# Loading a 1.2 KB input on the SyncE queue behind a 5 MB weight, instead of on the ScalarE queue at the same time

## Chip, cores, metric

The kernel runs on one core of a Trainium2 chip. The metric is the device time of one execution in microseconds (us), median of several runs. Times inside a trace are us from the start of the span.

## The reference, cut to what matters

One decode step of a transformer block: attention over a cache and a gated feed-forward, both on the layernormed input, summed with the input.

```python
x  = A_x                                     # [1, 1, 640] bf16: 1.2 KB
xn = layernorm(x)
# A: 32 heads, head size 128, 32768 cached positions each
q  = xn @ wq                                 # wq [640, 4096]: 5 MB
p  = softmax(q · k_cache * 128**-0.5)        # k_cache: 32 heads x 8 MB
A  = (p @ v_cache) @ wo                      # v_cache: 32 heads x 8 MB
# B: (silu(xn @ w_gate) * (xn @ w_up)) @ w_down
out = x + A + B
```

Nearly all of the 554 MB that the kernel reads is the cache. Loading it needs nothing of x, but no score can be computed before q.

## The kernel before

Every large input goes through a ring of three slots in SBUF. SyncE issues all large loads in one fixed order: wq, k0, k1, v0, k2, v1, ... (k0 is the k cache of head 0), then the feed-forward weights and wo. A load is issued as soon as its slot's last user is done. wq takes slot 0, k0 slot 1, k1 slot 2, and v0 takes slot 0 again: it waits until the q matmuls have read wq.

```python
ahead(lambda: nc.sync.dma_start(wq, A_wq...).then_inc(s_wq, 16))          # ahead of the start barrier
ahead(lambda: nc.scalar.dma_start(xrow, A_x[0, 0:1, :]).then_inc(s_x, 16))
...
@block.sync                                                               # after the start barrier
def sp(e):
    owner = {}                                                            # slot -> (semaphore, count) that frees it
    for u in units:
        s = slot_of[u]
        if s in owner:
            e.wait_ge(*owner.pop(s))
        if u[0] == "wq":
            owner[s] = (s_q, NQB)                                         # freed by the 8 groups of q matmuls
        elif u[0] == "k":
            e.dma_start(ring[:, s, :], kv_src(A_k_cache, u[1], 0, NJ)).then_inc(s_slot[s], 16)
            owner[s] = (s_qk, NHF * (u[1] + 1))                           # freed by that head's score matmuls
        ...
        elif u[0] == "v":
            e.dma_start(ring[:, s, :], kv_src(A_v_cache, u[1], 0, NJ)).then_inc(s_slot[s], 16)
            owner[s] = (s_pv, u[1] + 1)
```

xrow lies in the unused part of slot 0, on one partition. The layernorm runs on PE, DVE and ACT; its last step is a DVE copy that spreads xn for the matmuls. Then come the q matmuls, the copies of q from PSUM on ACT, and the first multiply:

```python
@block.tensor
def pe(t):
    t.wait_ge(s_x, 16)
    ... # two transposes of x, two sums of the layernorm
    t.wait_ge(s_a, 11)                     # DVE: xn is spread
    t.wait_ge(s_wq, 16)
    for b in range(NQB):                   # NQB = 8
        for c in range(NCD):
            mm = t.matmul(bank[b], lhsT=xnb[:, c, :], rhs=wq_v[:, c, b * 512:(b + 1) * 512], ...)
        mm.then_inc(s_q, 1)
    t.wait_ge(s_qc, NQB)                   # ACT: all 8 copies of q done
    ... # head after head: scores, softmax sums, p @ v

@block.vector
def dve(v):
    ... # layernorm
    step(v.tensor_copy(out=xnb[:, :, :], in_=xn[:, :, None].to_broadcast([128, NCD, 128])))
    v.wait_ge(s_qc, 1)                     # ACT: first copy of q done
    ... # per head: wait for its k load, four multiplies k * q, reductions, softmax
```

Of the kernel before, what the change touches and what calls it, by code (L numbers as in the profile page):

```python
# [12 lines left out]
def bass_parallel_sum__gqa_block_cached__swiglu_ffn__decode_kernel(  # L13
# [65 lines left out]
    with ExitStack() as es:  # L79
# [3 lines left out]
        def sem(name):  # L83
            return es.enter_context(nc.semaphore(name))
# [33 lines left out]
        s_x, s_wq, s_out = sem("x"), sem("wq"), sem("o")  # L118
# [20 lines left out]
        xrow = flat[0:1, x0 + NCD * 128:x0 + NCD * 128 + D]  # L139
# [5 lines left out]
        def ahead(start):  # L145

            at_start = nc.main_func.blocks[0]
            n = len(at_start.instructions)
            start()
            ins = list(at_start.instructions)  # L150
            new = ins[n:]
            drain = next(i for i, x in enumerate(ins)
                         if x.engine == new[0].engine and type(x).__name__ == "InstDrain")
            at_start.instructions = ins[:drain] + new + ins[drain:n]

        ahead(lambda: nc.sync.dma_start(wq, A_wq.rearrange("(p c) n -> p (c n)", c=NCD)).then_inc(s_wq, 16))
        ahead(lambda: nc.scalar.dma_start(xrow, A_x[0, 0:1, :]).then_inc(s_x, 16))
        block = es.enter_context(nc.Block(no_gpsimd_drain=True))
        f0 = FFN_S * CE
        wg = flat[:, f0:f0 + NCD * F]  # L160
# [23 lines left out]
        def kv_src(cache, h, j0, n):  # L184
            return cache[0, h].rearrange("(p j) d -> p (j d)", p=128)[:, j0 * DH:(j0 + n) * DH]
# [20 lines left out]
        with nc.psum_tensor("ps8", [128, 8, 512], F32) as ps8:  # L206
# [10 lines left out]
            @block.sync  # L217
            def sp(e):
                owner = {}
                for u in units:  # L220
                    s = slot_of[u]
                    if s in owner:
                        e.wait_ge(*owner.pop(s))
                    if u[0] == "wq":
                        owner[s] = (s_q, NQB)
                    elif u[0] == "k":
                        e.dma_start(ring[:, s, :], kv_src(A_k_cache, u[1], 0, NJ)).then_inc(s_slot[s], 16)
                        owner[s] = (s_qk, NHF * (u[1] + 1))
                    elif u == LASTV:
                        j = 0  # L230
                        for i, n in enumerate(TAIL):
                            e.dma_start(ring[:, s, j * DH:(j + n) * DH],
                                        kv_src(A_v_cache, u[1], j, n)).then_inc(s_tail[i], 16)
                            j += n
# [3 lines that stand above are left out]
                    elif u[0] == "ffn":  # L238
                        e.dma_start(wg, B_w_gate.rearrange("(p c) n -> p (c n)", c=NCD)).then_inc(s_ffn[0], 16)
                        e.dma_start(wu, B_w_up.rearrange("(p c) n -> p (c n)", c=NCD)).then_inc(s_ffn[1], 16)  # L240
                        e.dma_start(flat[:, d0:d0 + FM * D], B_w_down[0:FM * 128, :].rearrange(
                            "(p j) n -> p (j n)", j=FM)).then_inc(s_ffn[2], 16)
                        e.dma_start(wdr, B_w_down[FM * 128:F, :].rearrange(
                            "f (t n) -> (f t) n", t=2)).then_inc(s_ffn[2], 16)
                    else:
                        wo_src = A_wo.rearrange("(p j) n -> p (j n)", j=OC)
                        j = 0
                        for i, n in enumerate(WTAIL):
                            e.dma_start(wo[:, j * D:(j + n) * D], wo_src[:, j * D:(j + n) * D]).then_inc(s_wo[i], 16)  # L249
                            j += n  # L250
                e.wait_ge(s_fin, 2)
                e.dma_start(out[0, 0:1, :].rearrange("o (c m) -> (o c) m", c=NCD), orow[:, :]).then_inc(s_out, 16)
# [399 lines left out]
```

## Time and profile before

| | before |
|---|---|
| time, median of 3 runs | 1287.27 us (1287.13 to 1287.53) |
| span of the profiled execution | 1285.6 us |
| read from memory | 554 MB, 431 GB/s over the span |
| busy: PE, DVE, ACT | 81%, 52%, 4% |

First the top of the profile page of before: busy time by engine (share of the span), then 40 equal slices of the span with the busy share of the DMA engines in tenths. PE is TensorE's matmuls, PEld its weight loads, DVE is VectorE, ACT ScalarE, POOL GpSimd; in the timelines SPq and ACTq are DMA issues of SyncE and ScalarE.

```profile
PE 1042.0 (81%) x5154; PEld 260.9 (20%) x3235; DVE 672.2 (52%) x409; ACT 52.1 (4%) x139; POOL 2.5 (0%) x17
...
DMA  9999999999999999999999999999999999999998
```

The DMA engines are at nine tenths or more in 39 of 40 slices. The compute engines are not full.

The start is where the change acts. The timeline of before gives, for each row: start in us, length in us, engine, source line, operation, and in brackets how long the engine had been idle and what ended that.

```profile
0.00 0.40 SPq L156 DMA_DIRECT2D ring<-in_A_wq_dram  x1
0.12 0.51 ACTq L157 DMA_DIRECT2D ring<-in_A_x_dram  x1
...
1.06 1.10 SPq L227 DMA_DIRECT2D ring<-in_A_k_cache_dram  x2
...
1.58 0.33 PE L282 MATMUL ps<-one,ring 1*128 1x1 bf16 x5 [1.58 <-DVE one L516]
...
5.67 0.82 DVE L535 COPY ring<-xn 128x640 bf16<-128x640 bf16 x1
...
15.35 10.43 PE L297 MATMUL ps<-ring 128*128 128x512 bf16 x39 [10.75 <-DMA ring<-in_A_wq_dram]
...
25.80 0.33 SPq L236 DMA_DIRECT2D ring<-in_A_v_cache_dram  x1
...
34.67 17.43 DVE L554 TENSOR_TENSOR ring<-ring,qb 128x8192 bf16<-128x8192 bf16 x4 [28.19 <-DMA ring<-in_A_k_cache_dram]
```

x is used from 1.58 us on. The layernorm runs while wq is being loaded and ends at 6.49 us. The q matmuls wait for wq until 15.35 us. v0 is issued at 25.80 us, when the q matmuls are done. The first multiply waits for k0 until 34.67 us: "idle 28.19" is the wait of DVE.

### The profile page before, as it was taken

The numbers are of one execution on the slowest core, as the hardware profiler recorded it, in microseconds if no ns is written. First come the engines' busy times: TensorE is split into PE (matmuls) and PEld (weight loads), VectorE is DVE, ScalarE is ACT, GpSimd is POOL, SyncE is SP. The second block draws the span as 40 slices with busy tenths as digits, with TensorE's granted clock in tenths as the row PEclk, the third lists the DMA queues.
The fourth block names the chain that finished last, engine by engine and source line by source line (L and its number), as shares of the span: only waits on it lengthen the run. The fifth ranks groups of instructions, "written<-read, shape, count | busy, mean of one in ns | idle before, by whom it ended". The sixth has DMA issues, their size and how long they took to land.

```text
span 1285.6 us, 9851 instructions
## 1 busy us (share of the span) xinstructions
PE 1042.0 (81%) x5154; PEld 260.9 (20%) x3235; DVE 672.2 (52%) x409; ACT 52.1 (4%) x139; POOL 2.5 (0%) x17
## 2 busy tenths in 40 slices
PE   3599777889787799778788777898777798778797
PEld 1012112221112221112221112221112221112227
DVE  0855665445665446664446664446664446654441
ACT  2000000000000000000000000000000000000000
POOL 0000000000000000000000000000000000000000
PEclk9799888999888898888998888998888998888995
DMA  9999999999999999999999999999999999999998
GB/s 424 425 445 433 427 430 441 428 432 440 432 432 428 440 430 430 442 430 432 428 440 430 430 442 430 432 428 440 430 430 442 430 432 428 440 430 430 442 413 365
DMA packets 11256, 554.17 MB, mean 431 GB/s; under 512 B 1259, under 2 KB 1516, under 8 KB 1772
## 3 DMA queue, kind: packets, MB, share of 16 engines
q1 hardware_dynamic: 11242, 554.00, 99.7%
q8 instruction: 9, 0.15, 0.0%
q14 instruction: 3, 0.02, 0.0%
q10 hardware_dynamic: 2, 0.00, 0.0%
HBM read 553.99 MB, written 0.00 MB: 431 GB/s over the span
## 4 chain that ended last, share of the span: by engine, by line
DMA 53%; PE 28%; DVE 12%; issue 6%; SPq 0%; DVEq 0%
DMA ring<-in_A_k_cache_dram 51%; PE ps L337 17%; DVE ring L554 12%; PE ps L305 9%; DMA ring<-in_A_wo_dram 2%; PE ps L324 1%; PE ps L379 0%; PE ps L373 0%; PE ps L367 0%; PE ps L428 0%; SPq L249 0%; DVEq L554 0%; DVE sc L560 0%; DVE pmax L566 0%; DVE m L569 0%
## 5 line engine op out<-in xcount | busy, mean ns | idle before, releaser
L554 DVE TENSOR_TENSOR ring<-ring,qb 128x8192 bf16<-128x8192 bf16 x128 | 557.8, 4420 | 315.6 <-DMA ring<-in_A_k_cache_dram 315.6
L305 PE MATMUL ps<-ring,ident 128*128 128x512 bf16 x1920 | 498.4, 418 | 0.0
L337 PE MATMUL ps<-ring,P 128*4 128x512 bf16 x1984 | 443.3, 379 | 0.0
L324 PE MATMUL ps<-ring,ident 128*128 128x512 bf16 x128 | 56.1, 439 | 220.1 <-DVE ring L554 219.7
L337 PEld LDWEIGHTS ps<-ring,P 128*4 128x4 bf16 x1984 | 163.4, 85 | 237.8
L324 PEld LDWEIGHTS ps<-ring,ident 128*128 128x128 bf16 x128 | 12.6, 99 | 618.3 <-DVE ring L554 359.5
L560 DVE TENSOR_REDUCE sc<-ps 128x64 f32<-128x512 f32 x128 | 82.2, 683 | 63.4 <-PE ps L305 63.4
L572 DVE TENSOR_SCALAR negb<-ps 128x1 f32<-128x1 f32 x32 | 5.1, 159 | 108.4 <-PE ps L379 108.4
L480 ACT ACTIVATE P<-sc,negb 128x256 bf16<-128x256 f32 x32 | 16.2, 507 | 957.7 <-DVE negb L572 957.7
L569 DVE TENSOR_REDUCE m<-ps 1x1 f32<-1x128 f32 x32 | 8.9, 279 | 85.2 <-PE ps L373 85.2
L359 PEld LDWEIGHTS ps<-identf,o 4*128 4x128 f32 x248 | 30.7, 190 | 13.1 <-issue 13.1
L359 PE MATMUL ps<-identf,o 4*128 4x1 f32 x248 | 33.3, 251 | 0.0
L367 PEld LDWEIGHTS ps<-rsum,ones 128*128 128x128 f32 x64 | 12.1, 190 | 99.7 <-issue 98.9
L471 ACT ACTIVATE o<-ps,rzb 4x512 f32<-4x512 f32 x31 | 21.0, 678 | 6.2 <-PE ps L337 6.2
L297 PE MATMUL ps<-ring 128*128 128x512 bf16 x39 | 10.4, 428 | 10.8 <-DMA ring<-in_A_wq_dram 10.7
L476 ACT ACTIVATE ocol<-ps 128x1 f32 (+1 forms) x31 | 5.4, 173 | 222.4 <-PE ps L359 222.4
L566 DVE TENSOR_REDUCE pmax<-sc 128x1 f32<-128x256 f32 x32 | 13.4, 420 | 0.0
L373 PE MATMUL ps<-identf,pmax 128*1 128x128 f32 x64 | 12.2, 273 | 1.2 <-DVE pmax L566 1.2
L379 PE MATMUL ps<-m,ones 1*128 1x1 f32 x64 | 12.1, 256 | 0.4 <-DVE m L569 0.4
L379 PEld LDWEIGHTS ps<-m,ones 1*128 1x128 f32 x64 | 9.4, 182 | 14.2 <-issue 13.5
L403 PE MATMUL ps<-xn,ring 128*128 128x1 bf16 x140 | 8.3, 196 | 1.3 <-issue 1.3
L542 DVE RECIPROCAL rzb<-ps 128x1 f32<-128x1 f32 x32 | 5.0, 157 | 8.1 <-PE ps L367 8.1
(66 smaller groups left out, 82.5 us busy)
## 6 DMA issues: line engine op xcount, KB each, us to landing
ring<-in_A_wq_dram SPq DMA_DIRECT2D x1, 5120.0 KB, 15.2
ring<-in_A_v_cache_dram SPq DMA_DIRECT2D x1, 4096.0 KB, 31.8
ring<-in_A_wo_dram SPq DMA_DIRECT2D x3, 1280.0 KB, 24.7
ring<-in_B_w_gate_dram SPq DMA_DIRECT2D x1, 2160.0 KB, 23.2
ring<-in_B_w_up_dram SPq DMA_DIRECT2D x1, 2160.0 KB, 27.9
ring<-in_B_w_down_dram SPq DMA_DIRECT2D x1, 2080.0 KB, 31.3
ring<-in_A_v_cache_dram SPq DMA_DIRECT2D x1, 2048.0 KB, 36.4
ring<-in_A_v_cache_dram SPq DMA_DIRECT2D x2, 1024.0 KB, 39.4
```

The source lines that it names most:

```text
L305: return t.add_instruction(mybir.InstMatmult(start_tensor_calc=False, stop_tensor_calc=stop, tile_size=(128, 128), tile_position=(0, 0), l ...
L324: t.matmul(ob, lhsT=ident[:, :], rhs=src, start=True, stop=False)
L337: mm = t.matmul(O, lhsT=P[:, h % PR, j:j + W], rhs=ring[:, s, j * DH:(j + W) * DH], start=(j == 0), stop=(j + W == NJ))
L359: mm = t.matmul(fold_ps, lhsT=o4[:, m * DH:(m + 1) * DH], rhs=identf[0:W, m:m + 1], start=(m == 0), stop=(m == W - 1))
L367: t.matmul(misc[:, 129:130], lhsT=ones[:, :], rhs=rsum[:, h % SR:h % SR + 1], start=True, stop=True).then_inc(s_z, 1)
L373: t.matmul(misc[0:1, 0:128], lhsT=pmax[:, h % SR:h % SR + 1], rhs=identf[:, :], start=True, stop=True).then_inc(s_t, 1)
L379: t.matmul(misc[:, 128:129], lhsT=ones[0:1, :], rhs=m1[0:1, h % SR:h % SR + 1], start=True, stop=True).then_inc(s_b, 1)
L471: a.activation(out=o4[:, :], in_=O, func=ACTF.Copy, scale=rzb[0:W, h % SR:h % SR + 1]).then_inc(s_o4, 1)
L480: a.activation(out=P[:, h % PR, :], in_=sc[:, :], func=ACTF.Exp, bias=negb[:, h % SR:h % SR + 1], scale=c_scale, accum_out=rsum[:, h % SR: ...
L554: v.tensor_tensor(out=kh, in0=kh, in1=q[:, None, :].to_broadcast([128, HF, DH]), op=ALU.mult).then_inc(s_mul, 1)
L560: v.tensor_reduce(out=sc[:, i * HF:(i + 1) * HF], in_=bank[i].rearrange("p (j e) -> p j e", e=G), axis=AX.X, op=ALU.add).then_inc(s_red, 1)
L566: v.tensor_reduce(out=pmax[:, h % SR:h % SR + 1], in_=sc[:, :], axis=AX.X, op=ALU.max).then_inc(s_max, 1)
```

## The change

The intent is to put x on the same queue as wq, directly behind it, so that ScalarE issues no DMA at all.

```diff
         ahead(lambda: nc.sync.dma_start(wq, A_wq.rearrange("(p c) n -> p (c n)", c=NCD)).then_inc(s_wq, 16))
-        ahead(lambda: nc.scalar.dma_start(xrow, A_x[0, 0:1, :]).then_inc(s_x, 16))
         block = es.enter_context(nc.Block(no_gpsimd_drain=True))
@@ in the SyncE program
                     if u[0] == "wq":
+                        e.dma_start(xrow, A_x[0, 0:1, :]).then_inc(s_x, 16)
                         owner[s] = (s_q, NQB)
```

It changes two things at once: the queue, and the moment of issue (behind the start barrier instead of ahead of it).

## The prediction

> **What bounds the kernel now.** The DMA engines. The page's slices show them at nine tenths or more in 39 of 40 slices, moving 431 GB/s; 554 MB at that rate is the whole span of 1285.6 us. PE is busy 81%, DVE 52% (busy table). From 100 to 1200 us the stage table has a DMA share of 1.00. The cache loads land a median 41.5 us (k) and 36.8 us (v) after issue (DMA issues), but one 8 MB load takes only about 19.4 us at 431 GB/s (worked out), so each is issued about one whole load ahead of its turn. The chain of waits ends in the wo loads and about 2.5 us of compute.
>
> **What the change does.** The same 1.2 KB is loaded, 1/430,000 of the traffic. Removed: one issue on ScalarE (0.51 us, timeline). Added: one issue on SyncE between wq and the first k load, 0.4 to 0.55 us like its neighbours. The first k load is then issued at about 1.6 us instead of 1.06, while wq (landing 15.2 us after issue) keeps the engines busy: no gap.
>
> Moved: the landing of x. Before, x was there by 1.55 us, and the layernorm ran hidden under the wq load: 1.55 to 6.49 us, 4.94 us. After, x lies behind wq. The Trainium skill ("DMA: Bandwidth & Descriptors", section "Queues, rings and completion order") says each DMA engine consumes its ring's descriptors in order, and that a semaphore increment lands only after that engine's earlier writes. So I expect x at about 15.5 us (14 to 17.5), about when wq lands. The trace of before doesn't show this order.
>
> The layernorm then stands exposed behind wq. Estimate: layernorm 15.5 to 20.5 us; first q matmul at 20.5 instead of 15.35; first qb copy done 2.9 us later, at 23.4 (before 18.27); all eight at 31.6 (before 26.41); the v load that waits for the q matmuls issued at about 31 instead of 25.80.
>
> **How much is on the critical path: none.** The next user of q is the first DVE multiply, which waited 28.2 us for the first k load, until 34.67 us. It needs only the first qb copy: 11 us of slack remain. PE needs all eight at its first score matmul at 39.21 us: over 7 us remain. The v load issued at 31 us has two 8 MB k loads ahead of it; the second lands at about 54 us (33.5 and about 52.5 us after issue), so the queue holds some 23 us of work and cannot run dry. The next k load waits for the first head's scores (issued 55.82), which don't move. From 34.67 us on both traces should be equal.
>
> **Prediction.** 1287.3 us, 8 times in 10 within 1286.2 to 1288.6. Faster by over 2%: 0.5%; within 2%: 98.5%; slower by over 2%: 1%.
>
> **What would show each step.** The x issue on SyncE's row near 1.06 us; first transpose matmul on x at 14 to 17.5 us; q matmuls starting 5 us later, released by DVE's copy and no longer by the wq load; ACT's qb copies and the v issue 5 us later; first DVE multiply still at 34.7 us, released by the k load; DMA share still near 0.97 between 25 and 55 us; the same GB/s and tail.
>
> **What would make it wrong.** x landing much later than wq (after about 26 us, for instance behind the k loads), which would delay the first multiply; a small transfer that stalls one DMA engine's stream for microseconds, shifting every later load; or a lower clock granted to PE. DVE sat idle about 9.7 us before each late k load (timeline), so a late start of some microseconds should be absorbed in a few heads.

## The result

| | before | after |
|---|---|---|
| time, median of 4 runs | 1287.20 us (1287.11 to 1287.53) | 1287.32 us (1287.19 to 1287.41) |
| ratio after / before | | 1.0, 95% interval 0.9983 to 1.0018 |
| span of the profiled execution | 1285.6 us | 1285.4 us |

A ratio here and below is the mean time of one kernel's fast runs over the mean of the other's fast runs of the same rounds, so it is not quite the ratio of the medians.

The top of the profile page of after is the same picture:

```profile
PE 1043.6 (81%) x5154; PEld 261.0 (20%) x3235; DVE 672.2 (52%) x409; ACT 52.1 (4%) x139; POOL 2.5 (0%) x17
...
DMA  9999999999999999999999999999999999999998
```

The timeline of after, the rows that answer to those of before:

```profile
0.00 0.39 SPq L156 DMA_DIRECT2D ring<-in_A_wq_dram  x1
...
0.80 0.30 SPq L224 DMA_DIRECT2D ring<-in_A_x_dram  x1
...
1.15 1.14 SPq L227 DMA_DIRECT2D ring<-in_A_k_cache_dram  x2
...
14.58 0.35 PE L282 MATMUL ps<-one,ring 1*128 1x1 bf16 x5 [14.58 <-DMA ring<-in_A_x_dram]
...
18.70 0.82 DVE L535 COPY ring<-xn 128x640 bf16<-128x640 bf16 x1
19.57 0.13 PEld L297 LDWEIGHTS ps<-ring 128*128 128x128 bf16 x2 [2.03 <-DVE ring L535]
19.58 10.63 PE L297 MATMUL ps<-ring 128*128 128x512 bf16 x39 [1.95 <-DVE ring L535]
...
30.24 0.33 SPq L236 DMA_DIRECT2D ring<-in_A_v_cache_dram  x1
...
34.82 17.43 DVE L554 TENSOR_TENSOR ring<-ring,qb 128x8192 bf16<-128x8192 bf16 x4 [15.30 <-DMA ring<-in_A_k_cache_dram]
```

The first use of x, q and the v0 issue are later; what follows is not, but for 0.15 us at first. x is used from 14.58 us on, 13 us later than before. The layernorm takes as long as it did (14.58 to 19.52 us, 4.94 us), but now it is exposed: the q matmuls start at 19.58 instead of 15.35 us, and what released them is DVE's copy of line 535, no longer the wq load. v0 is issued at 30.24 instead of 25.80 us. But the first multiply still starts when k0 lands, at 34.82 instead of 34.67 us; DVE was idle 15.30 us before it instead of 28.19 us. The difference of 0.15 us does not last: k3 is still issued 0.15 us later (94.20, before 94.05), and the load behind it, v2, no longer (114.41, before 114.47). It is also within the scatter of the profiles: in delay10 and v_late below, which issue x in the same place, the first multiply starts at 34.66 and 34.54 us.

### The profile page after: what moved, and what is told of

Same layout as the page of the kernel before. It is cut to its first block, busy times and chain, and to the rows that moved or that the text cites. A ratio compares the mean times of both kernels' runs of the same rounds, so it can differ in the third digit from the quotient of the medians.

```text
span 1285.4 us, 9851 instructions
## 1 busy us (share of the span) xinstructions
PE 1043.6 (81%) x5154; PEld 261.0 (20%) x3235; DVE 672.2 (52%) x409; ACT 52.1 (4%) x139; POOL 2.5 (0%) x17
## 4 chain that ended last, share of the span: by engine, by line
DMA 53%; PE 27%; DVE 13%; issue 6%; SPq 0%; DVEq 0%
DMA ring<-in_A_k_cache_dram 51%; PE ps L337 17%; DVE ring L554 13%; PE ps L305 8%; DMA ring<-in_A_wo_dram 2%; PE ps L324 1%; PE ps L379 0%; PE ps L373 0%; PE ps L367 0%; PE ps L428 0%; SPq L249 0%; DVEq L554 0%; DVE sc L560 0%; DVE pmax L566 0%; DVEq L196 0%
## 6 DMA issues: line engine op xcount, KB each, us to landing
ring<-in_A_wq_dram SPq DMA_DIRECT2D x1, 5120.0 KB, 15.4
```

## The experiments

The theory to test: the layernorm's move is free because it fits into slack, and that slack has a definite size, set by how long the DMA queue holds work. The rivals: the lateness is free at any size, because idle time of DVE absorbs it later; or the equality is a cancellation of a gain and a loss; or it holds only because the first multiply did not move. All kernels gave a correct result. "Cost" is the median of the kernel minus the median of before on the same chip.

| label | v0 issued | first multiply | cost | ratio to before, 95% interval |
|---|---|---|---|---|
| after (4 runs) | 30.24 | 34.82 | +0.1 us | 0.9983 to 1.0018 |
| delay10 | 40.63 | 34.66 | −0.1 us | 0.9985 to 1.0013 |
| x_behind_k0 | 50.77 | 42.28 | +0.3 us | 0.9989 to 1.0016 |
| delay25 | 54.90 | 46.67 | +4.0 us | 1.0015 to 1.0042 |
| delay30 | 58.23 | 50.95 | +7.8 us | 1.0048 to 1.0079 |
| x_behind_k1 | 69.80 | 61.66 | +18.5 us | 1.0129 to 1.0160 |
| v_late | 59.19 | 34.54 | +8.6 us | 1.0052 to 1.0080 |
| dve_late | 30.53 | 49.05 | +4.1 us | 1.0018 to 1.0045 |
| delay30_v_early | 59.21 (two thirds) | 50.85 | +7.2 us | 1.0041 to 1.0068 |

Times in columns two and three are us from the start of the span, read from each kernel's timeline.

### delay10: q ten microseconds later

The last copy of the layernorm is repeated; each repeat takes 0.86 us.

```diff
-                step(v.tensor_copy(out=xnb[:, :, :], in_=xn[:, :, None].to_broadcast([128, NCD, 128])))
+                for _ in range(12):
+                    step(v.tensor_copy(out=xnb[:, :, :], in_=xn[:, :, None].to_broadcast([128, NCD, 128])))
```

(The count that PE waits for grows with it.)

> The kernel after, with DVE's last copy of the layernorm (0.86 us each) repeated 11 more times: q about 9.5 us later. Slack theory: first q matmul at about 29.0 us instead of 19.6, first qb copy done at 32 us, still before the first k load (34.8), so the first DVE multiply stays at 34.8; the v issue moves from 30.2 to about 39.7 us, the queue still holds work until about 54 us. Total unchanged, within 1 us of before. Rival 'delay of q is paid in full': about 9.5 us more. Rival 'PE must have all qb copies by 39.4 us': all eight at about 40.3 us, which would show as 1 us on the first score matmul but not in the total.

Measured: 1287.28 us against 1287.42 us for before. The timeline has the v0 issue and the first multiply:

```profile
34.66 17.43 DVE L555 TENSOR_TENSOR ring<-ring,qb 128x8192 bf16<-128x8192 bf16 x4 [5.49 <-DMA ring<-in_A_k_cache_dram]
...
40.63 0.33 SPq L236 DMA_DIRECT2D ring<-in_A_v_cache_dram  x1
```

The first multiply stayed where k0 lands (34.66 us). PE's first score matmul did have to wait for the last copy of q: it began at 41.29 instead of 39.39 us, later than the estimate of 40.3 us. That was made up inside the same head: the next k load, which waits for that head's scores, was issued at 55.81 us (after: 55.96).

### x_behind_k0 and x_behind_k1: x further back in the same queue

```diff
                     if u[0] == "wq":
-                        e.dma_start(xrow, A_x[0, 0:1, :]).then_inc(s_x, 16)
                         owner[s] = (s_q, NQB)
                     elif u[0] == "k":
                         e.dma_start(ring[:, s, :], ...).then_inc(s_slot[s], 16)
+                        if u[1] == 0:          # x_behind_k1: == 1
+                            e.dma_start(xrow, A_x[0, 0:1, :]).then_inc(s_x, 16)
```

> x issued on SyncE behind the first k load instead of ahead of it: x lands at about 34 us, q matmuls from 39, v issue at about 49.6 us, first DVE multiply at about 42 instead of 34.8 us. Slack theory (the DMA queue is what counts): queue holds work until about 54 us, so no DMA gap and total within 1 us of before although DVE and PE start 7 us late; the lateness is worked off in DVE's idle time before the following k loads within a few heads. Rival 'equal only because the first multiply does not move': about 7 us more.

> x issued behind both first k loads: x lands at about 53.5 us, v issue at about 69 us. Slack theory: DMA gap from about 54 to 70 us, total 15 to 18 us above before (1302 to 1305 us); against delay30 the v issue moves 10.4 us later and the total must move by the same 10.4 us (slope one beyond the edge). Rival 'absorbed': no difference. Rival 'paid in full': 39 us more.

x_behind_k0 measured 1287.75 us against 1287.42 us, no difference outside the interval, although the first multiply came 7.5 us late. The timeline shows that lateness being worked off. These are the rows of the multiplies of the heads 0 to 4 (start, length, and idle time before):

```profile
42.28 17.43 DVE L555 TENSOR_TENSOR ring<-ring,qb 128x8192 bf16<-128x8192 bf16 x4 [3.21 <-ACT qb L463]
...
67.89 17.43 DVE L555 TENSOR_TENSOR ring<-ring,qb 128x8192 bf16<-128x8192 bf16 x4
...
97.00 17.43 DVE L555 TENSOR_TENSOR ring<-ring,qb 128x8192 bf16<-128x8192 bf16 x4 [0.16 <-issue]
...
133.17 17.43 DVE L555 TENSOR_TENSOR ring<-ring,qb 128x8192 bf16<-128x8192 bf16 x4 [7.15 <-DMA ring<-in_A_k_cache_dram]
...
171.87 17.43 DVE L555 TENSOR_TENSOR ring<-ring,qb 128x8192 bf16<-128x8192 bf16 x4 [9.75 <-DMA ring<-in_A_k_cache_dram]
```

In after the same groups start at 34.82, 58.41, 93.20, 132.22 and 170.96 us. The lateness shrinks from 7.5 over 9.5 and 3.8 to 0.9 us in the fourth and fifth head. So "equal only because the first multiply did not move" falls.

x_behind_k1 measured 1305.90 us, 18.5 us more, slightly above the expected 15 to 18. So "free at any size" falls too. x landed with the second k load: it was first used at 53.52 us. Windows of x_behind_k1 (columns: window, its length, busy time and instruction count of each engine, granted TensorE clock, DMA share, GB/s) show the DMA engines empty until v0 comes. (A DMA share above 1.00 comes from the tool, which books a packet in the window in which it starts.)

```profile
50.00:60.00 10.00, 3.15 (x18) 1.99 (x19) 2.33 (x11) 0.20 (x1) 0.00 (x0) 1.00 0.24 105
60.00:70.00 10.00, 9.77 (x37) 3.86 (x35) 8.34 (x2) 4.37 (x8) 0.00 (x0) 1.00 0.00 0
70.00:80.00 10.00, 9.54 (x45) 0.29 (x3) 10.00 (x5) 1.69 (x2) 0.00 (x0) 1.00 1.03 419
80.00:90.00 10.00, 5.20 (x25) 0.48 (x5) 5.52 (x7) 0.60 (x2) 0.00 (x0) 0.87 0.97 419
```

### delay25 and delay30: where the slack ends

The same repeated copy, 29 and 34 times instead of 12.

> The layernorm's last copy repeated 28 more times, so q is about 23.9 us later and the v issue comes at about 54.0 us, just before the second k load's completion is seen (53.5 to 54). Theory that the queue must be refilled about 3 us before that (edge at a v issue of about 51 us, worked out from delay30 and x_behind_k1): total about 3 us (2 to 4) above before. Prediction as put on record (the queue holds work until 54 us, no cost before that): 0 to 1 us above before.

> The same with 33 more copies: q about 28.4 us later, v issue at about 58.6 us. Slack theory: the second k load ends at about 54 us and the queue is empty until the v issue plus about 1 us to the first byte: a DMA gap of 5 to 7 us, and the total is 5 to 7 us above before, 1292 to 1294 us. Rival 'paid in full': 28 us more. Rival 'absorbed by later idle time of DVE': no difference.

delay25 cost 4.0 us and delay30 7.8 us, at v0 issues of 54.90 and 58.23 us; x_behind_k1 cost 18.5 us at 69.80 us. Subtracting the cost from the moment of the v0 issue gives 51.0, 50.4 and 51.3 us: in these runs, beyond an edge at about 51 us each microsecond costs a microsecond, and x_behind_k0 at 50.77 us lies at the edge and cost 0.3 us. (delay25 and delay30_v_early varied by about 2 us from run to run, delay25 from 1289.96 to 1292.02 us; the other kernels by at most 1.3 us.) delay30 cost more than the 5 to 7 us expected, because the expectation still put the edge at 54 us; the expectation of delay25 was written after delay30 and x_behind_k1 and used the edge at 51 us. The prediction had the queue hold work until 54 us, when the second k load has landed; for delay25 that meant a cost of 0 to 1 us, and it cost 4.0 us. The edge lies about 2.5 us before the moment at which the end of the second k load is seen (53.5 us, from x_behind_k1). About 1 us of that passes between the issue and the first packet: in delay30 v0 is issued at 58.23 us and the first packet starts between 59.1 and 59.2 us, in v_late 59.19 us and between 60.1 and 60.2 us. What the rest consists of, no run resolves.

### delay30_v_early: a longer queue, the same late q

This was meant to prove that delay30 lost its time to the empty queue. The last third of v0 goes to a part of slot 0 that wq, x and xn do not use, so it can be issued without waiting for q.

```diff
                     elif u[0] == "k":
                         e.dma_start(ring[:, s, :], ...).then_inc(s_slot[s], 16)
+                        if u[1] == 1:
+                            e.dma_start(ring[:, WQ_S, J0 * DH:CE], kv_src(A_v_cache, 0, J0, NJ - J0)).then_inc(s_v0, 16)
...
                     elif u[0] == "v":
-                        e.dma_start(ring[:, s, :], kv_src(A_v_cache, u[1], 0, NJ)).then_inc(s_slot[s], 16)
+                        n = J0 if u[1] == 0 else NJ
+                        e.dma_start(ring[:, s, 0:n * DH], kv_src(A_v_cache, u[1], 0, n)).then_inc(s_slot[s], 16)
```

(J0 is 170 of 256 blocks; PE also waits for s_v0 before it uses v0.)

> delay30 with the last 86 of 256 column blocks of the first v load (the part of the slot that wq, x and xn do not use, 2.8 MB) issued right behind the second k load, without waiting for q; q stays as late as in delay30. Theory that delay30 lost its time because the DMA queue ran dry: the early piece is 6.5 us of work at 433 GB/s, the queue lasts to about 60 us, the v issue at about 58.2 us finds it nearly full: total 0 to 2 us above before, 6 to 8 us below delay30. Rival 'delay30 lost its time because the first multiply and PE started 16 us late': as delay30, about 7.8 us above before.

The expectation failed: 1294.48 us, 7.2 us above before, about as slow as delay30. The theory as stated, with the v0 issue as the only limit, falls. Windows of delay30, and then of delay30_v_early, show why (columns as above):

```profile
50.00:60.00 10.00, 9.31 (x42) 3.50 (x35) 9.05 (x3) 5.92 (x9) 0.00 (x0) 1.00 0.56 211
60.00:70.00 10.00, 10.00 (x48) 0.29 (x3) 10.00 (x5) 0.14 (x1) 0.00 (x0) 1.00 0.95 413
70.00:80.00 10.00, 3.80 (x19) 0.48 (x5) 6.29 (x7) 0.60 (x2) 0.00 (x0) 0.92 0.98 421
...
90.00:100.00 10.00, 10.00 (x49) 1.86 (x21) 5.73 (x7) 0.00 (x0) 0.00 (x0) 1.00 0.98 419
```

```profile
50.00:60.00 10.00, 9.31 (x37) 3.67 (x34) 9.15 (x3) 4.94 (x9) 0.00 (x0) 1.00 0.91 387
60.00:70.00 10.00, 10.00 (x47) 0.20 (x2) 9.48 (x4) 1.12 (x1) 0.00 (x0) 1.00 1.04 418
70.00:80.00 10.00, 4.62 (x22) 0.48 (x5) 5.82 (x6) 0.60 (x2) 0.00 (x0) 0.85 0.88 349
...
90.00:100.00 10.00, 9.29 (x45) 1.50 (x16) 6.71 (x7) 0.00 (x0) 0.00 (x0) 1.00 0.79 315
```

The early piece did fill most of the gap at 50 to 60 us (211 became 387 GB/s). But the queue then ran low at 70 to 80 us (349 instead of 421 GB/s) and at 90 to 100 us (315 instead of 419 GB/s). The next two loads wait for the scores of head 0 and head 1, and those were as late as in delay30: the SyncE rows show k2 issued at 73.89 us and v1 at 97.48 us (delay30: 72.91 and 96.50 us). So there is a second limit: a late first multiply makes the loads behind v0 late. If there are two limits in delay30, taking one away would only expose the other. The next two runs take them apart.

### v_late and dve_late: one limit at a time

v_late makes only the v0 issue late; dve_late makes only the first multiply late.

```diff
# v_late
                     if u[0] == "wq":
                         e.dma_start(xrow, A_x[0, 0:1, :]).then_inc(s_x, 16)
-                        owner[s] = (s_q, NQB)
+                        owner[s] = (s_exp, 1)
# dve_late
-                v.wait_ge(s_qc, 1)
+                v.wait_ge(s_qc, NQB)
+                for n in range(4):
+                    v.tensor_reduce(out=pmax[:, 2:3], in_=qb[:, :], axis=AX.X, op=ALU.max).then_inc(s_late, 1)
+                    v.wait_ge(s_late, n + 1)
                 for h in range(H0):
```

> The kernel after, with one edit: the first v load waits for the first head's softmax (seen at 58.9 us) instead of for the q matmuls. q, the first DVE multiply (34.8 us), the scores and the second head are as early as in after; only the v issue is late, at about 59 us, as in delay30. Theory 'queue run dry by the late v issue' (cost begins at a v issue of about 51 us): total 7 to 9 us above before. Rival 'delay30 paid for the late start of DVE and PE, not for the v issue': 0 to 1 us above before. Both may be true in delay30: then this run shows the v issue alone suffices.

> The kernel after, with four reductions of all of qb into an unused column (about 4.3 us each) on DVE between the last qb copy and the first multiply: q, the qb copies and the v issue (30 us) stay as early as in after, only DVE's first multiply is late, at about 48 us. In delay30_v_early the third v-or-k pair behind it came late: the k load waits for the first head's scores (22 us after the first multiply), the next v load for the second head's (45.6 us after it), and x_behind_k0 shows no cost with that v issue at 89.0 us. Theory 'late start of DVE is a second limit of its own': next v issue at about 94 us, total 3 to 6 us above before, DMA share below 0.97 between 90 and 100 us. Rival 'only the first v issue counts, the rest is worked off in idle time': 0 to 1 us above before.

The rows of v_late, and then of dve_late:

```profile
34.54 17.43 DVE L554 TENSOR_TENSOR ring<-ring,qb 128x8192 bf16<-128x8192 bf16 x4 [15.11 <-DMA ring<-in_A_k_cache_dram]
...
59.19 0.33 SPq L236 DMA_DIRECT2D ring<-in_A_v_cache_dram  x1
```

```profile
30.53 0.33 SPq L237 DMA_DIRECT2D ring<-in_A_v_cache_dram  x1
...
49.05 17.43 DVE L555 TENSOR_TENSOR ring<-ring,qb 128x8192 bf16<-128x8192 bf16 x4
...
93.79 0.33 SPq L237 DMA_DIRECT2D ring<-in_A_v_cache_dram  x1
```

Both came as the theory says. v_late cost 8.6 us with the first multiply on time (34.54 us), so the v0 issue alone suffices; if each microsecond costs a microsecond, 59.19 minus 8.6 gives 50.6 us, the same edge. (SyncE issues in a fixed order, so k2 comes late too, at 59.56 instead of 55.96 us, but right behind v0.) dve_late cost 4.1 us with the v0 issue on time (30.53 us), so the late multiply alone suffices too; v1 was issued at 93.79 us, and 93.79 minus 4.1 gives a second edge, at a v1 issue of about 89.7 us. That edge rests on this one run and on the same assumption of a microsecond for a microsecond. x_behind_k0, with v1 at 89.04 us, lies on its free side. In delay30 the two limits were passed by nearly the same amount: v0 by 58.23 minus 51, about 7 us, and v1 by 96.50 minus 89.7, about 7 us as well. The two do not add up to 14 us: after the gap at v0 all traffic is that much later, and the window of 90 to 100 us shows no second gap in delay30 (419 GB/s). So the rising cost in the delay runs can't be given to one of the two alone; that the first edge is where the delay runs put it is supported by v_late, in which the second limit is not passed (v1 at 79.86 us). Windows of v_late and then of dve_late show the gap in a different place:

```profile
50.00:60.00 10.00, 6.72 (x32) 0.47 (x5) 6.79 (x9) 0.60 (x2) 0.00 (x0) 0.93 0.25 107
...
90.00:100.00 10.00, 5.80 (x27) 2.12 (x25) 0.00 (x0) 0.68 (x1) 0.00 (x0) 0.98 1.06 459
```

```profile
50.00:60.00 10.00, 6.38 (x20) 0.20 (x2) 10.00 (x3) 0.00 (x0) 0.00 (x0) 0.60 1.09 472
...
90.00:100.00 10.00, 9.87 (x48) 3.02 (x34) 3.30 (x8) 0.00 (x0) 0.00 (x0) 1.00 0.57 223
```

That the cost is the time in which the DMA engines had no work can be checked by counting bytes in the traces. From 50 to 150 us the core moved 438 GB/s in before, and less in the runs that cost time. The last column is what the missing bytes are worth at the steady 433 GB/s:

| label | GB/s, 50 to 150 us | cost | missing bytes |
|---|---|---|---|
| delay25 | 419 | 4.0 us | 4.4 us |
| delay30 | 406 | 7.8 us | 7.4 us |
| x_behind_k1 | 356 | 18.5 us | 18.9 us |
| v_late | 399 | 8.6 us | 9.0 us |
| dve_late | 419 | 4.1 us | 4.4 us |
| delay30_v_early | 403 | 7.2 us | 8.1 us |

They agree to a microsecond, which is about what the edges of the window allow.

### x_act_in_block: undo the queue, keep the later issue

```diff
-                        e.dma_start(xrow, A_x[0, 0:1, :]).then_inc(s_x, 16)      # SyncE
 def act(a):
+                a.dma_start(xrow, A_x[0, 0:1, :]).then_inc(s_x, 16)
```

> x back on the ScalarE queue, but issued behind the start barrier (about 0.8 us) instead of ahead of it; one part of the change undone. x lands at about 2 us and the layernorm is hidden under wq again (q matmul at about 15.4 us). Theory that the barrier is passed at about 0.8 us instead of 1.06 us because ScalarE has no issue ahead of it: first k issue at about 0.80 us here too; if SyncE's own queue was the reason, it is back at 1.06. Total within 1 us of before in either case.

Measured: 1287.25 us against 1287.42 us. The first k load was issued at 0.82 us; in before, with ScalarE's issue ahead of the barrier, at 1.06 us. After also issues its first post-barrier DMA at 0.80 us. That agrees with the barrier being passed earlier when ScalarE has no issue ahead of it. One number missed: x was expected at about 2 us and was first used at 6.96 us, 6.15 us after its issue.

### x_act_late and x_act_late_ksplit: x on the other queue when the engines are busy

```diff
-                        e.dma_start(xrow, A_x[0, 0:1, :]).then_inc(s_x, 16)      # SyncE
 def act(a):
+                a.wait_ge(s_wq, 16)
+                a.dma_start(xrow, A_x[0, 0:1, :]).then_inc(s_x, 16)
```

x_act_late_ksplit does the same and also cuts k0 and k1 into four loads each, so that every partition's row is 16 KB instead of 64 KB.

> x on the ScalarE queue, issued only when wq has landed (about 15.3 us), when SyncE's queue already holds two k loads of 8 MB. Theory that each queue has its own ring and the engines alternate: x lands about 2 us after its issue, at 17 to 18.5 us, q matmuls from about 22.5, v issue at about 33 us, total within 1 us of before. Rival 'DMA engines serve transfers in order of issue across queues': x lands at about 53.5 us, v issue at about 69 us, total about 16 us above before, as when x is put behind both k loads on SyncE.

> x_act_late with the first two k loads each cut into four issues of a quarter of every partition's row (16 KB instead of 64 KB per row). x took 9.0 us from issue to first use in x_act_late and 6.2 us in x_act_in_block (rows of 40 KB). Theory that x waits for a few packets of the other queue already in hand on its DMA engine, whose time goes with the row's size: 2.5 to 4.5 us from issue to first use here. Rival 'a fixed delay of a second queue under load': 6 to 9 us again. Total within 1 us of before in either case.

x_act_late: 1287.37 us, no difference. The order-of-issue rival falls, because x did not wait for the k loads, which ended at about 54 us. But x was slower than expected: issued at 15.22 us, first used at 24.20 us, 9.0 us later. x_act_late_ksplit: 1287.77 us against 1287.33 us, and x was used 4.4 us after its issue. The timelines of the two, the issue of x and the first matmul on it:

```profile
15.22 0.51 ACTq L457 DMA_DIRECT2D ring<-in_A_x_dram  x1
...
24.20 0.35 PE L281 MATMUL ps<-one,ring 1*128 1x1 bf16 x5 [24.20 <-DMA ring<-in_A_x_dram]
```

```profile
15.27 0.51 ACTq L465 DMA_DIRECT2D ring<-in_A_x_dram  x1
...
19.65 0.35 PE L289 MATMUL ps<-one,ring 1*128 1x1 bf16 x5 [19.65 <-DMA ring<-in_A_x_dram]
```

The wait grows with the size of the other queue's rows, though not in proportion: 9.0 us at 64 KB, 6.2 us at 40 KB (x_act_in_block, beside wq), 4.4 us at 16 KB, from one profile each. An estimate from 433 GB/s over 16 engines is 2.4 us for one 64 KB row on one engine. So x may wait for some rows that the engine already has in hand; it does not wait for its turn in the order of issue. The rows in hand are a reading that fits; no run shows the inside of an engine.

### x_17_times: what a small transfer costs the stream

```diff
                         e.dma_start(xrow, A_x[0, 0:1, :]).then_inc(s_x, 16)
+                        for i in range(16):
+                            e.dma_start(spare[:, i * D:(i + 1) * D], A_x[0, 0:1, :]).then_inc(s_x, 16)
```

(spare is an unused piece of slot 0; PE waits for all 17.)

> The kernel after with 16 more loads of the same 1.2 KB behind x, all waited for. Theory that a small transfer in the stream costs next to nothing: the first k load lands at most 2.5 us later than 34.7 us (16 times the 0.15 us seen in the after trace is 2.4), the total is 0 to 2 us above before. Rival 'a small transfer stalls one engine's stream for about a microsecond': first k load at 50 us or later and total 13 us or more above before. SyncE spends about 5 us more on issues, so the first k issue moves to about 6.5 us, still under wq.

Measured: 1287.91 us against 1287.42 us, +0.5 us for 16 more transfers, ratio 1.0005 (0.9992 to 1.0019). The first multiply came at 36.24 instead of 34.82 us, that is 0.09 us for each added transfer:

```profile
17.62 0.35 PE L286 MATMUL ps<-one,ring 1*128 1x1 bf16 x5 [17.62 <-DMA ring<-in_A_x_dram]
...
36.24 17.43 DVE L558 TENSOR_TENSOR ring<-ring,qb 128x8192 bf16<-128x8192 bf16 x4 [13.68 <-DMA ring<-in_A_k_cache_dram]
```

(The 17 copies together were usable at 17.62 us, the one of after at 14.58 us: 0.19 us for each added one.) So the equality of before and after is no cancellation of a costly transfer against something else: one such transfer in the stream makes the next load about a tenth of a microsecond later.

## Why the prediction was right

**The bound.** Right. The DMA engines are full in both kernels (from 25 to 55 us, where x, q and v0 moved, the DMA share was 0.98 before and 1.01 after), and time appears only in runs where the windows show them without work, by about as much as the missing bytes are worth.

**x lands about when wq does.** Right in kind: 14.57 us (expected 15.5, range 14 to 17.5), and 13 us later than before. x was even a little earlier than the whole of wq (15.4 us). The prediction rested on the Trainium skill ("DMA: Bandwidth & Descriptors", section "Queues, rings and completion order"): each engine takes its ring's descriptors in order. After, x_behind_k0 and x_behind_k1 agree: x is first used at 14.58, 34.14 and 53.52 us when it is put behind wq and no, one or two k loads. That it beats the last part of wq fits the same page's section "Why a DMA increments its semaphore by 16 and not by 1", by which a DMA runs on up to 16 engines that finish independently, and only the engines that it uses have to finish. The packet counts agree that x uses few: the page of before lists two packets on x's queue, so at most two of the 16 engines carry it, while each of the six additional k loads of x_act_late_ksplit added 144 packets, which is one for each of 128 rows and 16 more.

**The layernorm is exposed, q moves by about 5 us.** Right. The layernorm took 4.94 us as before. The q matmuls moved by 4.23 us (predicted 5.15), v0 by 4.44 us (predicted 5.2), because x came 0.9 us earlier than estimated.

**The first k issue at 1.6 us.** Wrong by half a microsecond, without effect: 1.15 us. The prediction added x's issue to SyncE and did not reckon that the barrier is passed earlier without ScalarE's issue ahead of it; in x_act_in_block, which has none there, the first issue behind the barrier came at 0.82 us.

**None of it on the critical path.** Right, and shown: delay10 adds 10 us on top for nothing.

**The size of the slack.** Mis-sized. The prediction had the queue hold "some 23 us of work" at the v0 issue, until 54 us. The runs put the edge at a v0 issue of about 51 us, so after has about 21 us of slack there (51 minus 30.24). What was left out is that the new load had to be issued about 2.5 us before the end of the last load in the queue was seen. Also, the prediction counted on DVE's idle time to absorb a late first multiply "of some microseconds". That holds at 7.5 us (x_behind_k0, no cost) and no longer at 14 us (dve_late, 4.1 us): it is a second, separate limit that the prediction did not put a number on. Of the three things that it said would make it wrong, the first was too strict: x landing at 34 us, behind a k load, did delay the first multiply and cost nothing clear of the noise.

**A small transfer does not stall the stream.** Right: in x_17_times the first multiply moved by about 0.09 us for each.

**The tail.** The last wo load lets PE go at 1281.85 us before and 1281.67 us after, and the spans are 1285.6 and 1285.4 us: 0.2 us, less than the runs of one kernel differ (0.4 us for before).

What stays open: whether a change of 0.1 us in either direction is real. The intervals are about 0.18% wide to either side, some 2.3 us. The second edge, at a v1 issue of about 89.7 us, was not mapped by further runs.

## What to carry to other kernels

When the DMA queue is the bound, ask of every change at the start: by when must the next load be issued so that the queue does not run dry? In these runs work that was late but inside that limit was free, and beyond it every microsecond counted about in full. Look for all such limits, not only the first: here a late load issue and a late first multiply each cost time on their own, and repairing one of them alone gained almost nothing. And prove a "no difference" by pushing the suspected delay until it does cost: the point where it begins measures the slack.

## What the Trainium skill lacked or had wrong

- "DMA: Bandwidth & Descriptors", sections "Queues, rings and completion order" and "Issuing engines are not separate DMA queues": the page says that an engine alternates between its queues packet by packet, and gives no time for what a small transfer waits on the second queue when the first is busy. Here it was 6.2 us beside rows of 40 KB, 9.0 us beside 64 KB and 4.4 us beside 16 KB. When x was issued 0.12 us after wq, as in before, it could be used 1.5 us after its own issue.
- "DMA: Bandwidth & Descriptors", section "Where 436 GB/s comes from": it says without a condition that for transfers from HBM to SBUF the HBM side (about 358 GB/s) binds. This core, the only one that the program uses, kept 433 GB/s from 100 to 1200 us in before and in after. The page's own measurement just above, 425 GB/s for a core alone, agrees, and it is there that the page ties 358 GB/s to two cores streaming; read by itself the sentence would have predicted a much longer kernel (554 MB at 358 GB/s is about 1550 us, an estimate).
- No page says how early a load must be issued to keep a queue full. In these runs the cost began at an issue about 2.5 us before the end of the last queued load was seen (51 against 53.5 us), of which about 1 us lay between the issue and the first packet (58.23 and 59.1 to 59.2 us in delay30).
